# A three-block attention and expert kernel on one core: the first two tiles' softmax weights scaled by a product with a diagonal, first weight pieces split by VectorE, and the third tile's searches held behind the second tile

## The chip, the cores and the metric

The kernel runs on one core of a Trainium2 chip. The metric is the device time of one launch in microseconds (us), as the median of several runs. A profile shows one execution of it, engine by engine: TensorE (PE, with its weight loads PEld), VectorE (DVE), ScalarE (ACT), GpSimd (POOL) and SyncE (SP), which issues the transfers.

## The reference, cut to what matters

```python
# q, k, v: (2, 8, 576, 64); x has 1152 tokens of 512
scores = 0.125 * q @ k.T
mask = scores >= (32nd largest of each row)
attn = softmax over the kept scores
x = (attn @ v), heads side by side            # 1152 x 512
P = Sinkhorn scaling of exp(x @ w_gate)        # 1152 x 8
out = sum over 8 experts e of P[:, e] * (relu(x @ w1[e]) @ w2[e])
h = out @ w_in;  return (h * tanh(softplus(h))) @ w_out
```

## The kernel before

The 1152 tokens are nine tiles of 128 rows, counted from 0, in three chunks: (0, 1), (2, 3) and (4 to 8). For every tile and head, `scores` (L234) makes 128 x 576 scores on TensorE and ScalarE copies them out. `threshold` searches the 32 largest on VectorE: four times MAX8 (L262) and between them MATCH_REPLACE8 (L270). `mask` keeps the scores above the last one, and the exponentials; the weights lie in `em`. `norm` makes `r`, the reciprocal of the row's sum, on VectorE (L308, L309), and ScalarE multiplies `em` by it (L310). `values` turns the weights with four transposes against an identity (L330), for two heads together with a fifth for the 64 keys left (L341), ScalarE copies the result to `at` (L333) and `at2` (L344), and the product `pv` with the values follows (L353, L360). From `pv` ScalarE makes a rounded high part `xh` and VectorE the rest `xl`; for tile 1 each pair of heads has its own quarter (L367, L368).

The experts' passes take weights in pieces. For each piece `load_piece` fetches two halves `wraw0` and `wraw1`, ScalarE rounds them to `wh0` and `wh1` (L529), and GpSimd subtracts to get `wl0` and `wl1` (L533; VectorE takes a part of these in the last chunk). Three buffers hold the raw halves of each kind, so that the raw half of a piece is fetched when the split of the third piece before it is done. TensorE makes `h` from `xh`, `xl` and the pieces (L650), ScalarE and VectorE split it into `hh` and `hl` (L548, L549), and two pieces later `y` follows (L627). Expert 0 is done for tile 0 alone while tile 1's attention runs (`h_a`, L724, `y_a`, L710); the first chunk's pass then begins with expert 1, whose pieces are called `c0e1_0`, `c0e1_1` and so on.

TensorE's order is written by hand: the attention of tiles 2 and on is laid between the experts' products. The other engines' orders are set by a scheduler from priorities and its own estimate of times. `after(a, b)` adds a rule that `a` comes behind `b` in that order. The scores of tiles 2 and 3 are made early and wait in `early` stores. Tile 2's first MAX8 of a head is held behind `xl` of tile 1: heads 0 and 1 behind the quarter of pair 2, the others behind that of pair 3.

Of the kernel before, what the change touches and what calls it, by code (L numbers as in the profile page):

```python
# [10 lines left out]
F32 = mybir.dt.float32  # L11
F32R = mybir.dt.float32r
U32 = mybir.dt.uint32
AF = mybir.ActivationFunctionType
# [5 lines left out]
P = 128  # L20
B, H, S, D = 2, 8, 576, 64
# [5 lines left out]
NC = DM // P  # L27
# [13 lines left out]
CHUNKS = [(0, 1), (2, 3), (4, 5, 6, 7, 8)]  # L41
# [8 lines left out]
HOLD, RATE = 8, 0.25  # L50
ALONE, ALONE_RATE = 1, 3.4
FILL_FROM = 11
ROUND_AFTER = {f"c0e{ALONE}_0": H - 1, f"c0e{ALONE}_2": "v"}


class Streams:
# [19 lines left out]
def attention_moe_moe2(ctx: ExitStack, tc: tile.TileContext, qT, kT, vm, vt, wg, wst, w64, out):  # L76
    nc = tc.nc
# [5 lines left out]
    def after(inst, earlier):  # L83

        tc.add_manual_dep(
            inst.ins,
            earlier.ins.name,
            mybir.DependencyInfo(mybir.DependencyClass.NoSync, mybir.DependencyReason.DATA),
            reason="order",
        )  # L90
# [22 lines left out]
    hp = pool("hp", LAG + 1, stack=att)  # L113

    with st("attn"):
        ident = const.tile([P, P], F32, name="ident")
# [11 lines left out]
    xh, xl = {}, {}  # L128
# [24 lines left out]
    qset, live, away = {}, {}, {}  # L153
# [99 lines left out]
    def threshold(t, h, on_pool):  # L253

        with st("attn"):
            s = live["s", t, h]
            top = small.tile([P, TOPK], F32, tag="top", name=f"top_{t}_{h}")
            w = sp.tile([P, S], F32, tag="w", name=f"w_{t}_{h}")
            src = s
            for i in range(TOPK // 8):  # L260
                g = top[:, 8 * i : 8 * i + 8]
                top8 = nc.vector.max(g, src)  # L262
                if i == 0 and t == CHUNKS[0][-1] + 1:
                    key = 2 if h < 2 else 3
                    if ("xl", key) in live:
                        after(top8, live["xl", key])
                    else:
                        live.setdefault(("held", key), []).append(top8)
                if i + 1 < TOPK // 8:
                    nc.vector.match_replace(w, g, src, NEG)  # L270
                    src = w
            live["top", t, h] = top
            if not on_pool:
                live["e", t, h] = exponential(t, h, sp.tile([P, S], F32, tag="e", name=f"e_{t}_{h}"), s, nc.vector)
        yield from ()
# [27 lines left out]
    def norm(t, h, on_pool):  # L303
        with st("attn"):
            em, sm = live["em", t, h], live.pop(("sm", t, h))
            r = small.tile([P, 1], F32, tag="r", name=f"r_{t}_{h}")
            with st("moe" if on_pool else "attn"):
                nc.vector.tensor_scalar(r, sm, EPS, None, op0=ALU.add)  # L308
                nc.vector.reciprocal(r, r)  # L309
            nc.scalar.activation(em, em, AF.Copy, scale=r)  # L310
        yield from ()

    def turned(t, i, name):
# [7 lines left out]
    def values(t, h):  # L321
# [3 lines left out]
        j = h % 2  # L325
        with st("attn"):
            em = live.pop(("em", t, h))
            tr = turned(t, h, f"tr_{t}_{h}")
            for c in range(4):
                nc.tensor.transpose(tr[:, c, :], em[:, j * D + c * P :][:, :P], ident)  # L330
            at = sp.tile([P, 4, P], F32, tag="at", name=f"at_{t}_{h}", bufs=2)
            with st("evict"):
                nc.scalar.activation(at, tr, AF.Copy)  # L333
            live["at", j] = at
# [3 lines left out]
        pair = h // 2  # L338
        with st("attn"):
            tr2 = turned(t, 1, f"tr2_{t}_{h}")  # L340
            nc.tensor.transpose(tr2[:, 0, :], live.pop(("pair", t, h - 1))[:, 4 * P : 5 * P], ident)  # L341
            at2 = sp.tile([P, P], F32, tag="at2", name=f"at2_{t}_{h}")
            with st("evict"):
                live["copied", t, "v"] = nc.scalar.activation(at2, tr2[:, 0, :], AF.Copy)  # L344
        yield
        with st("attn"):
# [3 lines left out]
            for b, c0, c1, _, _ in queries(t, h // HG):  # L350
                for c in range(4):
                    for i in range(2):
# [4 lines left out]
                            start=(c == 0),  # L357
                            stop=False,
# [4 lines left out]
            ci, i = place[t]  # L363
            if t == CHUNKS[0][-1]:
                with st("first"):
                    hi, lo = (x[:, pair, i * P : (i + 1) * P] for x in x_tiles(ci))
# [4 lines left out]
            elif h == H - 1:  # L371
# [4 lines left out]
                hi, lo = (x[:, :, i * P : (i + 1) * P] for x in x_tiles(ci))  # L376
# [145 lines left out]
    def load_piece(tag, p, bufs2):  # L522
        res = []
        for a, (wp_a, bufs) in enumerate(((wp, 4), (wp if wq is None else wq, bufs2))):
            raw = wp.tile([P, DM], F32, tag=f"wraw{a}", name=f"wraw{a}_{tag}", bufs=3)
            nc.sync.dma_start(raw, p[:, a * DM : (a + 1) * DM])
            hi = wp_a.tile([P, DM], F32R, tag=f"wh{a}", name=f"wh{a}_{tag}", bufs=bufs)
            lo = wp_a.tile([P, DM], F32R, tag=f"wl{a}", name=f"wl{a}_{tag}", bufs=bufs)
            rounded = nc.scalar.activation(hi, raw, AF.Copy)  # L529
            if tag in ROUND_AFTER:  # L530
                after(rounded, live["copied", CHUNKS[0][-1], ROUND_AFTER[tag]])
            eng = nc.vector if (a and ps_b is not None) else nc.gpsimd
            eng.tensor_sub(lo, raw, hi)  # L533
            res.append((hi, lo))
        return res

# [403 lines left out]
```

## Time and profile before

| | us |
|---|---|
| median of 3 runs | 1217.76 |
| lowest, highest | 1215.89, 1219.01 |
| the profiled execution | 1214.06 |
| its span from first to last instruction | 1212.3 |

| engine | busy us | share of the span |
|---|---|---|
| TensorE | 1165.1 | 96% |
| VectorE | 853.6 | 70% |
| ScalarE | 652.9 | 54% |
| GpSimd | 514.2 | 42% |

The table of stages tells more than these shares: a stage is bounded by the engine that is busy all of it, or by the wait that ends last in it. In the timeline each row is a run of equal instructions on an engine: start, duration, what it is, and in brackets how long the engine idled before it and which instruction ended that. A row's duration includes the fill of the engine's pipeline, so equal rows overlap a little.

### The profile page before, as it was taken

What the parts mean: (1) busy time and instruction counts of PE and PEld (TensorE: products, weight loads), DVE (VectorE), ACT (ScalarE), POOL (GpSimd) and SP (SyncE); (2) the same over time, 40 slices, a digit from 0 to 9 for tenths busy, and PEclk for the clock granted to TensorE, in tenths of its full rate; (3) what the DMA queues carried; (4) which work ended last, traced back from release to release, by engine and by line L of the source; (5) the groups of instructions that cost most, each with busy time, mean ns of one, the idle gap of its engine ahead of it and who ended that gap; (6) DMA issues with size and microseconds to landing.
All of it is one profiled execution on the core that took longest, in us unless ns stands there. A gap on an engine that the chain in (4) does not pass through costs nothing.

```text
span 1212.3 us, 21068 instructions
## 1 busy us (share of the span) xinstructions
PE 1165.1 (96%) x7419; PEld 1042.2 (86%) x7419; DVE 853.6 (70%) x1868; ACT 652.9 (54%) x1305; POOL 514.2 (42%) x406
## 2 busy tenths in 40 slices
PE   3778999999999999999999999999999999999998
PEld 2556888988989899988999999999999999999997
DVE  7999999999999999913656868687576533333221
ACT  5877777876778777743223333333333334554432
POOL 6545778878787776752112121121211122221210
PEclk9999999999999999999999999999999999999999
DMA  8358566557665555544235666655444332223201
GB/s 251 115 184 261 177 184 183 175 179 222 186 201 164 159 167 164 176 144 144 71 94 177 201 189 196 195 183 182 151 140 147 119 102 64 88 96 117 76 27 44
DMA packets 105834, 184.68 MB, mean 152 GB/s; under 512 B 14208, under 2 KB 24704, under 8 KB 105728
## 3 DMA queue, kind: packets, MB, share of 16 engines
q1 hardware_dynamic: 104432, 182.15, 48.3%
q8 instruction: 58, 0.95, 0.3%
q10 hardware_dynamic: 1296, 1.18, 0.3%
q14 instruction: 48, 0.39, 0.1%
HBM read 159.43 MB, written 23.86 MB: 151 GB/s over the span
## 4 chain that ended last, share of the span: by engine, by line
PE 87%; DVE 6%; DMA 3%; ACT 2%; POOL 1%; issue 1%; SPq 0%; POOLq 0%; ACTq 0%
PE y_c2e L627 18%; PE h_c2e L650 18%; PE h_d L650 8%; PE y_d L627 8%; PE h_c1e L650 8%; PE y_c1e L627 8%; PE y_c0e L627 5%; PE h_c0e L650 5%; DVE top L262 3%; PE pv L353 2%; DMA kraw<-in_kT_dram 2%; PE tr L330 2%; DVE w L270 2%; PE sc L234 2%; PE pv L360 1%; DVE em L299 1%
## 5 line engine op out<-in xcount | busy, mean ns | idle before, releaser
L533 POOL TENSOR_TENSOR wl_c2e<-wraw_c2e,wh_c2e 128x512 fp32r<-128x512 f32 x64 | 84.2, 1316 | 348.4 <-ACT wh_c2e L529 348.4
L533 POOL TENSOR_TENSOR wl_c1e<-wraw_c1e,wh_c1e 128x512 fp32r<-128x512 f32 x128 | 171.2, 1348 | 60.1 <-ACT wh_c1e L529 57.2
L529 ACT ACTIVATE wh_c2e<-wraw_c2e 128x512 fp32r<-128x512 f32 x128 | 80.9, 632 | 194.6 <-PE y_c2e L627 100.6
L533 POOL TENSOR_TENSOR wl_c0e<-wraw_c0e,wh_c0e 128x512 fp32r<-128x512 f32 x112 | 149.9, 1356 | 42.1 <-ACT wh_c0e L529 37.7
L262 DVE MAX8 top<-w 128x8 f32<-128x576 f32 x216 | 158.6, 750 | 1.0
L650 PE MATMUL h_c2e<-xh,wh_c2e 128*128 128x256 f32 (+1 forms) x512 | 157.6, 308 | 1.3 <-DVE hl_c2e L549 1.3
L650 PE MATMUL h_c2e<-xl,wh_c2e 128*128 128x256 f32 (+1 forms) x512 | 157.1, 307 | 0.0
L650 PE MATMUL h_c2e<-xh,wl_c2e 128*128 128x256 f32 (+1 forms) x512 | 157.0, 307 | 0.0
L549 DVE SCALAR_TENSOR_TENSOR hl_c2e<-h_c2e,hh_c2e 128x256 fp32r<-128x256 f32 (+1 forms) x128 | 62.5, 489 | 98.9 <-ACT hh_c2e L548 98.4
L627 PE MATMUL y_c2e<-wh_c2e,hl_c2e 128*128 128x512 f32 x320 | 126.0, 394 | 0.0
L627 PE MATMUL y_c2e<-wh_c2e,hh_c2e 128*128 128x512 f32 x320 | 125.4, 392 | 0.0
L627 PE MATMUL y_c2e<-wl_c2e,hh_c2e 128*128 128x512 f32 x320 | 125.4, 392 | 0.0
L533 POOL TENSOR_TENSOR wl_d<-wraw_d,wh_d 128x512 fp32r<-128x512 f32 x32 | 41.5, 1296 | 160.5 <-ACT wh_d L529 160.5
L270 DVE MATCH_REPLACE8 w<-top,w 128x576 f32<-128x576 f32 x144 | 106.8, 743 | 0.0
L529 ACT ACTIVATE wh_c1e<-wraw_c1e 128x512 fp32r<-128x512 f32 x128 | 80.5, 629 | 47.2 <-PE y_c1e L627 22.0
L585 DVE TENSOR_TENSOR hl_d<-mg_d,hh_d 128x256 fp32r<-128x256 f32 x64 | 38.5, 602 | 91.9 <-ACT hh_d L584 91.9
L650 PEld LDWEIGHTS h_c2e<-xh,wh_c2e 128*128 128x128 f32 x512 | 96.2, 188 | 3.9 <-DVE hl_c2e L549 1.5
L650 PEld LDWEIGHTS h_c2e<-xl,wh_c2e 128*128 128x128 f32 x512 | 96.4, 188 | 2.5
L650 PEld LDWEIGHTS h_c2e<-xh,wl_c2e 128*128 128x128 f32 x512 | 96.2, 188 | 0.0
L529 ACT ACTIVATE wh_c0e<-wraw_c0e 128x512 fp32r<-128x512 f32 x112 | 70.1, 629 | 42.8 <-PE y_c0e L627 17.2
L234 PE MATMUL sc<-ks,q 128*128 128x288 f32 x320 | 65.3, 335 | 24.2 <-ACT s L243 4.9
L548 ACT ACTIVATE hh_c2e<-h_c2e 128x256 fp32r<-128x256 f32 (+1 forms) x128 | 54.7, 427 | 53.6 <-PE h_c2e L650 49.8
(171 smaller groups left out, 3313.8 us busy)
## 6 DMA issues: line engine op xcount, KB each, us to landing
wraw_c1e<-in_wst_dram SPq DMA_DIRECT2D x128, 256.0 KB, 3.0
wraw_c2e<-in_wst_dram SPq DMA_DIRECT2D x128, 256.0 KB, 3.0
wraw_c0e<-in_wst_dram SPq DMA_DIRECT2D x112, 256.0 KB, 3.0
cx<-in_w_dram SPq DMA_DIRECT2D x32, 512.0 KB, 4.2
wraw_d<-w SPq DMA_DIRECT2D x64, 256.0 KB, 2.6
yd<-ysp SPq DMA_DIRECT2D x32, 256.0 KB, 3.7
yb<-yd SPq DMA_DIRECT2D x32, 256.0 KB, 3.2
w<-cc SPq DMA_DIRECT2D x32, 256.0 KB, 3.5
```

The lines of the kernel that those rows point to most:

```text
L234: nc.tensor.matmul(halves[half], q[:, h % HG, :], ks[b, h][:, half * HS : (half + 1) * HS], start=(i == 0), stop=(i == len(terms) - 1),)
L262: top8 = nc.vector.max(g, src)
L270: nc.vector.match_replace(w, g, src, NEG)
L330: nc.tensor.transpose(tr[:, c, :], em[:, j * D + c * P :][:, :P], ident)
L353: nc.tensor.matmul(pv[i * D : (i + 1) * D, pair, c0:c1], vmain[b, pair][:, i, c, :], live["at", i][:, c, c0:c1], start=(c == 0), stop=False,)
L529: rounded = nc.scalar.activation(hi, raw, AF.Copy)
L533: eng.tensor_sub(lo, raw, hi)
L548: nc.scalar.activation(h, ps, AF.Relu)
L549: live["hl"] = nc.vector.scalar_tensor_tensor(l, ps, 0.0, h, op0=ALU.max, op1=ALU.subtract)
L585: nc.vector.tensor_sub(l, g, h)
L627: nc.tensor.matmul(y, h[:, j * P : (j + 1) * P], w, start=(f == 0 and k == 0), stop=(f == nf - 1 and k == 2),)
L650: nc.tensor.matmul(ps, w[:, c * P : (c + 1) * P], x[:, c, c0 : c0 + m], start=(k == 0), stop=(k == 3 * NC - 1),)
```

## The change

The kernel after differs in three things. For tiles 0 and 1, ScalarE no longer multiplies the weights by `r`; it multiplies the identity by it, which gives a 128 x 128 diagonal `turn`, and TensorE takes products of the weights with that diagonal where it took transposes. The fifth transpose of a pair becomes two products of 64 rows each. The order of expert 1's first three pieces is fixed anew: the subtractions for the first half of each go to VectorE, behind tile 1's last reciprocal; the roundings of the second halves, and of the third piece's first half, go behind tile 1's last copy, that of pieces 0 and 1's first halves behind the last head's copy of scores. And every first MAX8 of tile 2 is held behind the last quarter of tile 1's `xl`.

```diff
-ROUND_AFTER = {f"c0e{ALONE}_0": H - 1, f"c0e{ALONE}_2": "v"}
+FIRST_PIECES = {f"c0e{ALONE}_{f}": f for f in range(3)}
...
                 if i == 0 and t == CHUNKS[0][-1] + 1:
-                    key = 2 if h < 2 else 3
-                    if ("xl", key) in live:
-                        after(top8, live["xl", key])
+                    if ("xl", NC - 1) in live:
+                        after(top8, live["xl", NC - 1])
                     else:
-                        live.setdefault(("held", key), []).append(top8)
+                        live.setdefault(("held", NC - 1), []).append(top8)
...
-                nc.vector.reciprocal(r, r)
-            nc.scalar.activation(em, em, AF.Copy, scale=r)
+                inv = nc.vector.reciprocal(r, r)
+            if (t, h) == (CHUNKS[0][-1], H - 1):
+                live["ends"] = inv
+            if t > CHUNKS[0][-1]:
+                nc.scalar.activation(em, em, AF.Copy, scale=r)
+            else:
+                if h % 2 == 0:
+                    live["turn", t, h] = hp.tile([P, 2 * P], F32, tag="hl", name=f"turn_{t}_{h}")
+                turn = live["turn", t, h - h % 2][:, h % 2 * P :][:, :P]
+                nc.scalar.activation(turn, ident, AF.Copy, scale=r)
...
-                nc.tensor.transpose(tr[:, c, :], em[:, j * D + c * P :][:, :P], ident)
+                part = em[:, j * D + c * P :][:, :P]
+                if t > CHUNKS[0][-1]:
+                    nc.tensor.transpose(tr[:, c, :], part, ident)
+                else:
+                    nc.tensor.matmul(tr[:, c, :], part, live["turn", t, h - j][:, j * P :][:, :P], start=True, stop=True)
...
+                for i in range(2):
+                    keys = slice(i * D, (i + 1) * D)
+                    nc.tensor.matmul(tr2[keys, 0, :], tail[:, keys], turn[:, i * P :][:, :P], start=True, stop=True)
...
-            if tag in ROUND_AFTER:
-                after(rounded, live["copied", CHUNKS[0][-1], ROUND_AFTER[tag]])
             eng = nc.vector if (a and ps_b is not None) else nc.gpsimd
-            eng.tensor_sub(lo, raw, hi)
+            if tag in FIRST_PIECES:
+                late = a or FIRST_PIECES[tag] == 2
+                after(rounded, live["copied", CHUNKS[0][-1], "v" if late else H - 1])
+            if tag in FIRST_PIECES and not a:
+                after(nc.vector.tensor_sub(lo, raw, hi), live["ends"])
+            else:
+                eng.tensor_sub(lo, raw, hi)
```

VectorE behind tile 1's last reciprocal (`r_1_7`), in the kernel before; `top_2_0` is tile 2's head 0, `xl0` the low part of tile 1, whose four quarters have one name:

```order
L309 RECIPROCAL r_1_7_1254<-r_1_7_1254 128x1
L368 TENSOR_TENSOR xl0_806<-pv_1_1065,xh0_805 128x128
L262 MAX top_2_0_1239<-early_xh2_326 128x8
L262 MAX top_2_1_1265<-early_xh2_326 128x8
L270 MATCH_REPLACE w_2_0_1240<-top_2_0_1239,early_xh2_326 128x576
L280 TENSOR_SCALAR nb_2_0_1249<-top_2_0_1239 128x1
L270 MATCH_REPLACE w_2_1_1266<-top_2_1_1265,early_xh2_326 128x576
L280 TENSOR_SCALAR nb_2_1_1275<-top_2_1_1265 128x1
L262 MAX top_2_0_1239<-w_2_0_1240 128x8
L262 MAX top_2_1_1265<-w_2_1_1266 128x8
L270 MATCH_REPLACE w_2_0_1240<-top_2_0_1239,w_2_0_1240 128x576
L368 TENSOR_TENSOR xl0_806<-pv_1_1065,xh0_805 128x128
```

The quarter of pair 2 comes first, then nine instructions of tile 2's search, then the quarter of pair 3. VectorE at the same place in the kernel after:

```order
L308 RECIPROCAL r_1_7_1269<-r_1_7_1269 128x1
L553 TENSOR_TENSOR wl0_c0e1_0_1326<-wraw0_c0e1_0_1323,wh0_c0e1_0_1325 128x512
L553 TENSOR_TENSOR wl0_c0e1_1_1355<-wraw0_c0e1_1_1352,wh0_c0e1_1_1354 128x512
L386 TENSOR_TENSOR xl0_814<-pv_1_1076,xh0_813 128x128
L553 TENSOR_TENSOR wl0_c0e1_2_1384<-wraw0_c0e1_2_1381,wh0_c0e1_2_1383 128x512
L386 TENSOR_TENSOR xl0_814<-pv_1_1076,xh0_813 128x128
L262 MAX top_2_0_1254<-early_xh2_327 128x8
L262 MAX top_2_1_1280<-early_xh2_327 128x8
L262 MAX top_2_2_1523<-early_xh2_327 128x8
L262 MAX top_2_3_1628<-early_xh2_327 128x8
L269 MATCH_REPLACE w_2_0_1255<-top_2_0_1254,early_xh2_327 128x576
L279 TENSOR_SCALAR nb_2_0_1264<-top_2_0_1254 128x1
```

Three subtractions for expert 1's pieces stand among the quarters, and all of tile 2's search behind the last of them. The next instruction there is the first `hl` of expert 1. ScalarE behind tile 1's last copy (`at2_1_7`), in the kernel before:

```order
L344 ACTIVATE at2_1_7_1294<-tr2_1_7_1292 128x128
L529 ACTIVATE wh0_c0e1_2_1367<-wraw0_c0e1_2_1365 128x512
L529 ACTIVATE wh1_c0e1_2_1373<-wraw1_c0e1_2_1371 128x512
L529 ACTIVATE wh0_c0e1_3_1404<-wraw0_c0e1_3_1402 128x512
L281 ACTIVATE e_2_0_1248<-early_xh2_326,nb_2_0_1249 128x576
L367 ACTIVATE xh0_805<-pv_1_1065 128x128
```

and in the kernel after:

```order
L362 ACTIVATE at2_1_7_1310<-tr2_1_7_1307 128x128
L547 ACTIVATE wh0_c0e1_2_1383<-wraw0_c0e1_2_1381 128x512
L547 ACTIVATE wh0_c0e1_3_1420<-wraw0_c0e1_3_1418 128x512
L547 ACTIVATE wh1_c0e1_0_1331<-wraw1_c0e1_0_1329 128x512
L547 ACTIVATE wh1_c0e1_1_1360<-wraw1_c0e1_1_1358 128x512
L547 ACTIVATE wh1_c0e1_2_1389<-wraw1_c0e1_2_1387 128x512
L385 ACTIVATE xh0_813<-pv_1_1076 128x128
```

Between the last copy and the rounding of the last quarter stand five roundings of weights where three and an exponential stood. TensorE's order is the same in both kernels, but for the operands of the changed products. GpSimd's first subtraction for expert 1 is `wl0_c0e1_3`.

## Rows read from the trace of the kernel before

**Rows 1.** Stages: us, then each engine's busy us, TensorE's clock, DMA share, GB/s.

```profile
core 0: us, PE busy (x) PEld busy (x) DVE busy (x) ACT busy (x) POOL busy (x), PEclk, DMA share, GB/s
60.00:91.00 31.00, 23.21 (x158) 18.34 (x158) 30.79 (x77) 24.75 (x59) 12.27 (x13) 1.00 0.59 188
91.00:101.00 10.00, 10.00 (x75) 7.80 (x74) 9.86 (x22) 7.21 (x17) 4.28 (x4) 1.00 0.74 233
127.00:210.00 83.00, 83.00 (x600) 73.86 (x601) 82.92 (x214) 61.49 (x122) 65.66 (x50) 1.00 0.60 182
210.00:1212.00 1002.00, 996.38 (x6286) 901.09 (x6284) 654.78 (x1377) 497.90 (x982) 376.53 (x286) 1.00 0.46 144
```

**Rows 2.** Timeline of TensorE, 90 to 127 us: start, us, instruction, [idle before, releaser].

```profile
96.93 1.05 PE L724 MATMUL h_a<-x_alone,wraw_a 128*128 128x128 f32 x8
...
102.37 1.09 PE L353 MATMUL pv<-at,vm 128*64 128x128 f32 x16
104.38 0.49 PE L360 MATMUL pv<-at,vt 128*128 128x128 f32 x2 [0.92 <-ACT at L344]
104.71 1.04 PE L330 MATMUL tr<-ident,em 128*128 128x128 f32 x8
...
106.06 1.57 PE L353 MATMUL pv<-at,vm 128*64 128x128 f32 x16 [0.20 <-ACT at L333]
...
107.89 1.04 PE L330 MATMUL tr<-ident,em 128*128 128x128 f32 x8
...
109.98 1.57 PE L353 MATMUL pv<-at,vm 128*64 128x128 f32 x16 [0.95 <-ACT at L333]
...
111.73 0.37 PE L650 MATMUL h_c0e<-xh,wh_c0e 128*128 128x256 f32 x1
...
114.44 0.39 PE L650 MATMUL h_c0e<-xl,wh_c0e 128*128 128x256 f32 x1 [1.04 <-DVE xl L368]
...
117.54 0.38 PE L650 MATMUL h_c0e<-xh,wh_c0e 128*128 128x256 f32 x1 [1.18 <-DVE nb L280]
...
126.85 0.38 PE L650 MATMUL h_c0e<-xh,wh_c0e 128*128 128x256 f32 x1 [0.77 <-DVE hl_c0e L549]
```

**Rows 3.** Timeline of VectorE, 99 to 118 us.

```profile
99.14 1.70 DVE L299 SCALAR_TENSOR_TENSOR em<-s,top,e 128x576 f32<-128x576 f32 x1
...
105.78 0.81 DVE L299 SCALAR_TENSOR_TENSOR em<-s,top,e 128x576 f32<-128x576 f32 x1
...
106.82 0.16 DVE L309 RECIPROCAL r<-r 128x1 f32<-128x1 f32 x1
108.95 0.29 DVE L368 TENSOR_TENSOR xl<-pv,xh 128x128 fp32r<-128x128 f32 x1 [1.98 <-ACT xh L367]
...
114.10 0.29 DVE L368 TENSOR_TENSOR xl<-pv,xh 128x128 fp32r<-128x128 f32 x1
...
117.06 0.43 DVE L549 SCALAR_TENSOR_TENSOR hl_c0e<-h_c0e,hh_c0e 128x256 fp32r<-128x256 f32 x1
```

**Rows 4.** Timeline of ScalarE, 103 to 113 us.

```profile
103.41 0.76 ACT L310 ACTIVATE em<-em,r 128x576 f32<-128x576 f32 x1
...
110.45 1.69 ACT L529 ACTIVATE wh_c0e<-wraw_c0e 128x512 fp32r<-128x512 f32 x3
...
112.68 0.28 ACT L367 ACTIVATE xh<-pv 128x128 fp32r<-128x128 f32 x1
```

**Rows 5.** The chain of waits in order of time: start, us, what.

```profile
52.62 0.66 ACT em L310
```

**Rows 6.** Transfers issued from 100 to 116 us: count, size, median us to landing.

```profile
wraw_c0e<-in_wst_dram SPq DMA_DIRECT2D x11, 256.0 KB, 5.3
```

**Rows 7.** Line L533 on VectorE: count, least, median and greatest ns, first and last start.

```profile
L533 DVE TENSOR_TENSOR wl_c2e<-wraw_c2e,wh_c2e x64: 680/686/693, 543.1 to 979.8; 128x512 fp32r<-128x512 f32 x64
```

**Rows 8.** Timeline at tile 3's first head, on VectorE and on TensorE.

```profile
183.79 0.14 DVE L309 RECIPROCAL r<-r 128x1 f32<-128x1 f32 x1
...
186.66 0.60 PE L330 MATMUL tr<-ident,em 128*128 128x128 f32 x4
```

More of the change, by code (lines that the diff above doesn't have):

```diff
@@ L340, in values @@
             tr2 = turned(t, 1, f"tr2_{t}_{h}")
-            nc.tensor.transpose(tr2[:, 0, :], live.pop(("pair", t, h - 1))[:, 4 * P : 5 * P], ident)
+            tail = live.pop(("pair", t, h - 1))[:, 4 * P : 5 * P]
+            if t > CHUNKS[0][-1]:
+                nc.tensor.transpose(tr2[:, 0, :], tail, ident)
+            else:
+                turn = live.pop(("turn", t, h - 1))
+                for i in range(2):
+                    keys = slice(i * D, (i + 1) * D)
+                    nc.tensor.matmul(tr2[keys, 0, :], tail[:, keys], turn[:, i * P :][:, :P], start=True, stop=True)
             at2 = sp.tile([P, P], F32, tag="at2", name=f"at2_{t}_{h}")
@@ L529, in load_piece @@
             rounded = nc.scalar.activation(hi, raw, AF.Copy)
-            if tag in ROUND_AFTER:
-                after(rounded, live["copied", CHUNKS[0][-1], ROUND_AFTER[tag]])
             eng = nc.vector if (a and ps_b is not None) else nc.gpsimd
-            eng.tensor_sub(lo, raw, hi)
+            if tag in FIRST_PIECES:
[3 more added lines that the diff above has]
+                after(nc.vector.tensor_sub(lo, raw, hi), live["ends"])
+            else:
+                eng.tensor_sub(lo, raw, hi)
             res.append((hi, lo))
```

## The prediction, as it was made before the result

> **What bounds the kernel now.** I read the table by stages first [rows 1]. From 210 us to the end TensorE is busy 996.4 of 1002 us, and from 127 to 210 us all of it; a change to the first two tiles can reach the end only by the moment at which TensorE gets into that stretch, or by a wait that it opens inside it. In the same 83 us from 127 to 210 VectorE is busy 82.9: it works on the searches of tiles 2 and 3 (tiles are counted from 0 here, so the "third tile" is tile 2) and has nothing to spare. From 91 to 101 us TensorE is full too (10.00 of 10), while from 60 to 91 it is busy 23.2 of 31.
>
> Then TensorE in order of time between 90 and 127 us [rows 2]: six waits, 0.92, 0.20, 0.95, 1.04, 1.18 and 0.77, 5.06 us together. They are all that the change can win there. Last VectorE and ScalarE in the same stretch [rows 3, 4]: the last reciprocal of tile 1 is made at 106.82, VectorE idles 1.98 us, makes one quarter of tile 1's low part at 108.95, then searches for tile 2 and only at 114.10 makes the last quarter, for which TensorE waits at 114.44.
>
> **Products instead of transposes.** Four transposes of a head are four instructions, four fp32 products are eight: eight of either take the same 1.04 and 1.05 us [rows 2], so each is near 0.11 us and a head costs 0.44 us more. The tail goes from one instruction to four of 64 rows; sixteen such take 1.09 us with their fill, so 0.26 instead of 0.11, +0.15 a pair (+0.33 if the halves don't overlap). For 16 heads and 8 pairs that is 7.0 + 1.2 = 8.2 us more TensorE work. Tile 0's half lies before 91 us, where TensorE idles 7.8 us of 31 [rows 1] and where waits for others end last: taken as nothing, at most 4.1. Tile 1's half is on the path.
>
> The Trainium skill, "TensorE: Matmul & The Clock Gate", section "Terms", calls the transpose mode 4x faster for FP32; the eight-instruction group of [rows 2] shows 2x for this shape, and I go by the row. By the page tile 1's heads would pay 1.32 instead of 0.44 each; that is a rival below.
>
> **Scaling a diagonal instead of the weights.** ScalarE gives up 0.76 us a head for 128 columns, which take it 0.28 [rows 4]: 0.5 us back, 16 times. Three of the old scalings of tile 0 stand in the chain of waits, the last of them at 52.62 [rows 5], so at most 1.5 us could be won ahead of 60 us. VectorE runs without a pause between there and 91, and TensorE is full from 91, with more work than before; I take 0.2.
>
> **Tile 1, step by step.** Heads 1 to 3 and two tails come ahead of the product for pair 1 that starts at 102.37: 3 x 0.44 + 2 x 0.15 = 1.62, so 103.99. Its length 1.09 ends at 105.08; the wait of 0.92 at 104.38 is gone, because the tail's copy stood behind a 0.76 scaling [rows 4]. Net +0.70. Heads 4, 5 and a tail add 1.03: the next product, 1.15 us after the transposes without its wait of 0.20, comes at 105.41 + 1.15 + 1.03 = 107.6 instead of 106.06; ScalarE's copy of the doubled head ends near 107.9, so between, 107.7. The next transposes come at 109.5 instead of 107.89; with 1.14 us (2.09 less the wait of 0.95) and 1.03 more, pair 3 starts at 111.7, and with the copy behind it about 111.8 instead of 109.98. Expert 1's first product then starts at 113.5 instead of 111.73, **+1.8 us**. Two of the waits vanish and the added work outweighs them.
>
> **ScalarE's queue in front of the last quarter.** After tile 1's last copy, at about 112.1, the order now holds five roundings of weight pieces and only then the rounding of the last quarter; before it held three and an exponential. Three took 1.69 [rows 4], five take 2.7: 114.8, then 0.28 and 0.29 for the high and low part [rows 3, 4]: 115.3. One of the five needs a raw piece that can be fetched only after VectorE's split at 107 (its buffer is freed by that), and a fetch takes 5.3 us in this stretch [rows 6]: 112.9, when its turn is at 112.6. Up to 1 us late; I take 115.5 for the end of the last quarter, bounds 114.3 (as now) and 116.4.
>
> **Splits on VectorE.** Three at 0.69 [rows 7], 2.1 us. Two lie in VectorE's present 1.98 us of idling, the third in the wait for ScalarE: nothing. If that cover were gone, 2.1. GpSimd's queue gets three subtractions shorter; the next pieces come no later for that.
>
> The Trainium skill, "GPSIMD Engine Reference", section "Key points", says that GpSimd shares its SBUF interfaces with VectorE and collides with instructions that have two SBUF inputs. Here a masking instruction beside a GpSimd subtraction took 1.70, and 0.81 alone [rows 3]; so the trace agrees. By it the third split could take 0.89 longer; the order of GpSimd has its first subtraction behind a rounding that comes after that split's, so I take nothing.
>
> **The held searches.** This is the term that decides. Before, the first search of tile 2 started right behind the quarter at 108.95, about 109.16, and between there and 114.10 VectorE did nine instructions of that search, seven of them long ones at about 0.69 us. Now all of tile 2 waits for the last quarter: 115.5 instead of 109.16, less the 0.19 of that quarter itself, which stood among them: VectorE is **6.15 us late** with tiles 2 and 3, and it has no idle time up to 210 to make it up [rows 1]. On VectorE the low part of expert 1's first piece now stands behind four maxima and one replacement (five at 0.69, 3.4 us), so 118.9 instead of 117.06 [rows 3]: TensorE's wait of 1.18 goes to the same kind of wait, 1.8 later.
>
> How late may VectorE be? Tile 3's first weights have their reciprocal at 183.93 and, with 0.77 for the scaling, stand ready 2.0 us ahead of TensorE at 186.66 [rows 8]. TensorE's order is unchanged there, so 6.15 - 2.0 = **4.15 us** of wait lands in a stretch where TensorE had none. The 1.8 us of the tile-1 part is not added: both measure the same lateness, and the larger rules. After 210 TensorE is full; with 0.2 from tile 0, +4.0.
>
> **Sum.** The profiled execution took 1214.06 us (span 1212.3 and 1.8 around it): 1214.06 + 4.0 = 1218.1. The median of the three runs, 1217.76, lies 3.7 above that execution; the same step on it gives **1221.8**. About 0.3% (3.65 us) is what a measurement of this kernel can tell from no change, so the forecast is a slight slowing at the edge of it.
>
> **Rivals.** A: VectorE's lateness is mostly swallowed. For: ScalarE's scalings of tiles 2 and 3 stand behind other work on its queue, so orders that shift a little can find slack, and GpSimd's shorter queue makes masking faster (up to 0.89 an instruction). With the last quarter at 114.3 lateness is 4.95; less 2.0 and 0.9 it costs 2, 1219.8: within 0.3%. Against: [rows 1] show no idle time. B, the other side: tile 1's part decides and VectorE doesn't. If the early 1.5 us carries to 91, all 5.06 us of waits go and only 1.62 of the products shows, the end comes 4.9 earlier, 1212.9. The point from which it decides is a lateness under 2.0, a last quarter before 111.4, when its product hasn't started; so hardly. C: lateness is paid twice, because expert 1's low parts stand in the same VectorE order as the searches and each late one stops TensorE as at 126.85: 6.15 without slack and 0.5 more, 1224.4. D: the product costs four times a transpose: seven heads at 0.88 more, +6.2, 1228; the row speaks against it. That the change doesn't do what it says is ruled out by the order, where splits, products and the hold all stand.
>
> **Chances.** Forecast 0.48, A 0.40, B 0.05, C 0.06, D 0.01. Slower by over 0.3%: forecast, C and D, 0.55; within: 0.40; faster: 0.05. The range reaches from just below no change, which holds A, to a little over C with the spread of the runs: 1217.4 to 1225.4.
>
> **What would show it.** Eight instructions for each head's product; VectorE idle about 7 us in all between 106 and 116, its first tile-2 search at 115 to 116; TensorE's waits at 104 and 110 gone, one of about 2 us before expert 1's third piece, and new waits of together some 3 us between 130 and 200 at the transposes of tiles 2 and 3 for ScalarE's scaling. After 210 the two traces should run at a constant distance. I am wrong if the searches start before 112, or if TensorE shows no new wait between 130 and 200.

## The result, and the profile after it

The changed kernel takes 1226.03 us (median of five runs, 1223.04 to 1229.25) against 1217.76 of the kernel before; these two medians differ by 8.3. The ratio on record is 1.0081, interval 1.0067 to 1.0096, so 8.2 to 11.7 us slower, 9.9 in the middle; the differences below are all taken from such ratios. The forecast was slower, by 4.0 us, 1221.8, and its range ended at 1225.4: the direction was right, the size less than half. (Below, a thousandth of the ratio is 1.2 us.) The profiled execution took 1228.52 us, span 1226.7.

The stages after, as [rows 1] before (us, then each engine's busy us with its instructions, TensorE's clock, DMA share, GB/s):

```profile
core 0: us, PE busy (x) PEld busy (x) DVE busy (x) ACT busy (x) POOL busy (x), PEclk, DMA share, GB/s
60.00:91.00 31.00, 24.49 (x166) 19.50 (x165) 29.45 (x74) 20.21 (x54) 13.48 (x12) 0.94 0.51 164
91.00:101.00 10.00, 8.99 (x68) 6.96 (x67) 8.28 (x21) 6.96 (x18) 1.80 (x2) 1.00 0.68 200
127.00:210.00 83.00, 77.18 (x540) 67.30 (x539) 82.99 (x196) 57.33 (x112) 62.59 (x48) 0.98 0.56 169
210.00:1226.00 1016.00, 1010.66 (x6386) 913.22 (x6384) 669.49 (x1418) 510.04 (x1002) 388.57 (x294) 1.00 0.46 144
```

From 127 to 210 us TensorE had 83.00 of 83 before; now it has 77.18, and part of that at a lower clock, while VectorE is as full as it was. From about 200 us on the two traces run at nearly a constant distance: the transposes that the kernel before makes at 202 us come 14.2 us later, its products at 451 us 14.9 and those at 565 us 14.4 us later (this execution is 2.5 us over its median, that of before 3.7 under).

TensorE at the places that the forecast named, as [rows 2] before:

```profile
113.43 1.09 PE L371 MATMUL pv<-at,vm 128*64 128x128 f32 x14 [0.17 <-ACT at L344]
...
118.73 0.36 PE L672 MATMUL h_c0e<-xh,wh_c0e 128*128 128x256 f32 x1
...
124.48 0.38 PE L672 MATMUL h_c0e<-xh,wh_c0e 128*128 128x256 f32 x1 [1.84 <-DVE hl_c0e L571]
...
140.74 0.29 PE L427 MATMUL lg<-ident,lt 16*128 16x16 f32 x2 [2.65 <-ACT lt L422]
140.96 0.78 PE L649 MATMUL y_c0e<-wh_c0e,hh_c0e 128*128 128x512 f32 x1
141.54 0.63 PE L649 MATMUL y_c0e<-wl_c0e,hh_c0e 128*128 128x512 f32 x1
...
145.26 0.66 PE L339 MATMUL tr<-ident,em 128*128 128x128 f32 x4 [1.39 <-ACT em L312]
```

The waits of 0.92 and 0.95 in tile 1 are gone but for 0.17, as foreseen; expert 1's first product stands at 118.73 instead of 111.73; the new wait before its third piece is 1.84. Then come two things that were not foreseen: a wait of 2.65 us at the gate's logits, and behind it a product of 512 columns that takes 0.63 to 0.78 us instead of 0.39. VectorE shows where the first comes from:

```profile
111.72 0.16 DVE L308 RECIPROCAL r<-r 128x1 f32<-128x1 f32 x1
...
115.28 0.29 DVE L386 TENSOR_TENSOR xl<-pv,xh 128x128 fp32r<-128x128 f32 x1 [2.21 <-ACT xh L385]
118.14 0.69 DVE L553 TENSOR_TENSOR wl_c0e<-wraw_c0e,wh_c0e 128x512 fp32r<-128x512 f32 x1 [2.56 <-ACT wh_c0e L547]
120.38 0.29 DVE L386 TENSOR_TENSOR xl<-pv,xh 128x128 fp32r<-128x128 f32 x1 [1.55 <-ACT xh L385]
120.59 2.73 DVE L262 MAX8 top<-early_xh 128x8 f32<-128x576 f32 x4
...
133.54 4.60 DVE L298 SCALAR_TENSOR_TENSOR em<-early_xh,top,e 128x576 f32<-128x576 f32 x1
...
138.80 0.80 DVE L298 SCALAR_TENSOR_TENSOR em<-early_xh,top,e 128x576 f32<-128x576 f32 x1
```

The hold is there: 6.3 us of idling, then the first search of tile 2 right behind the last quarter. But the masking of tile 2's head 0 takes 4.60 us, the next one 0.80. GpSimd and ScalarE in the same stretch:

```profile
118.70 18.82 POOL L555 TENSOR_TENSOR wl_c0e<-wraw_c0e,wh_c0e 128x512 fp32r<-128x512 f32 x15 [14.46 <-ACT wh_c0e L547]
139.56 1.28 POOL L555 TENSOR_TENSOR wl_c0e<-wraw_c0e,wh_c0e 128x512 fp32r<-128x512 f32 x1 [2.04 <-ACT wh_c0e L547]
```

```profile
138.18 0.78 ACT L280 ACTIVATE e<-early_xh,nb 128x576 f32<-128x576 f32 x1 [2.91 <-DVE em L298]
...
140.33 0.36 ACT L422 ACTIVATE lt<-lt 16x256 f32<-16x256 f32 x1
```

GpSimd stands for 14.46 us, because its first subtraction's rounded piece now comes behind the end of tile 1; then it has 15 subtractions in a row, up to 118.70 + 18.82 = 137.52. The masking that starts at 133.54 ends at 138.14, 0.62 us after the row. ScalarE's next exponential waits 2.91 for it, the copy of the gate's logits stands behind that exponential, and TensorE waits for the copy. The granted clock then is 0.50, the lower level of 1.2 GHz:

```profile
140.00:141.00 1.00, 0.26 (x3) 0.23 (x3) 1.00 (x4) 1.00 (x3) 0.84 (x1) 1.00 0.00 0
141.00:144.00 3.00, 2.87 (x7) 1.76 (x6) 3.00 (x10) 0.64 (x4) 1.28 (x1) 0.50 0.45 102
```

So there were two questions: which part of the change costs how much, and how much of it is this masking.

### The profile page after: what moved, and what is told of

Its sections match the earlier page's. It is cut to its first block, busy times and chain, and to the rows that moved or that the text cites. A ratio compares the mean times of both kernels' runs of the same rounds, so it can differ in the third digit from the quotient of the medians.

```text
span 1226.7 us, 21247 instructions
## 1 busy us (share of the span) xinstructions
PE 1178.6 (96%) x7507; PEld 1053.4 (86%) x7507; DVE 859.4 (70%) x1871; ACT 650.2 (53%) x1305; POOL 511.2 (42%) x403
## 4 chain that ended last, share of the span: by engine, by line
PE 84%; DVE 7%; ACT 2%; issue 1%; DMA 1%; POOL 0%; ACTq 0%; POOLq 0%; SPq 0%
PE y_c2e L649 18%; PE h_c2e L672 18%; PE h_d L672 8%; PE y_d L649 8%; PE h_c1e L672 8%; PE y_c1e L649 8%; PE y_c0e L649 4%; PE h_c0e L672 4%; DVE top L262 2%; PE pv L371 2%; DVE w L269 2%; PE tr L339 2%; PE sc L234 2%; DVE em L298 1%; PE pv L378 1%
## 5 line engine op out<-in xcount | busy, mean ns | idle before, releaser
L555 POOL TENSOR_TENSOR wl_c0e<-wraw_c0e,wh_c0e 128x512 fp32r<-128x512 f32 x109 | 146.3, 1361 | 54.9 <-ACT wh_c0e L547 48.6
```

## Experiments

**The changed kernel again**, for a second profile.

> The changed kernel once more, for a second profile of it. The first profile showed the distance to the kernel before grow in three places: +1.9 us at 76 us (tile 0), +4.9 at 91 us (a wait of 2.12 us and a stretch of half clock behind it), +7.0 at expert 1's first product, and +8 more between 130 and 175 us, where one masking took 4.60 us beside 15 GpSimd subtractions in a row and the granted clock was 0.50 for some 3 us. If these belong to the kernel, the second profile has them at the same instructions: masking of tile 2's head 0 over 3 us, GpSimd without a subtraction from 104 to 118. If they belong to that one execution (its 1228.5 us is 2.5 over the median), the masking takes 0.8 to 1.9 us and the distance after 175 us is 9 to 11 us. Time by either: 1226, between 1223 and 1229.

Measured: 1227.2 us, ratio 1.0081 (1.0062 to 1.0099). The second profile has the same masking, wait and clock (0.50 from 139 to past 144 us), so they belong to the kernel:

```profile
116.99 2.73 DVE L262 MAX8 top<-early_xh 128x8 f32<-128x576 f32 x4
...
129.92 4.60 DVE L298 SCALAR_TENSOR_TENSOR em<-early_xh,top,e 128x576 f32<-128x576 f32 x1
```

```profile
137.11 0.29 PE L427 MATMUL lg<-ident,lt 16*128 16x16 f32 x2 [2.56 <-ACT lt L422]
```

What differs are the first 110 us: expert 1 starts 3.6 us earlier here, and 1.7 of that are there at 62 us already, where the second profile is as early as that of the kernel before. The distance of the first profile at 119 us is therefore not all the change's; against the kernel before, the second has expert 1's first product 3.40 us later (115.13 and 111.73).

**The three parts, alone and left out.** only_H is the kernel before with the hold, only_P with the products, only_S with the splits (the held roundings belong to them); no_P, no_H and no_S are the changed kernel with one part undone.

```diff
# only_H, on the kernel before
-                    key = 2 if h < 2 else 3
-                    if ("xl", key) in live:
+                    if ("xl", NC - 1) in live:
...
# no_H, on the changed kernel: the same lines back
```

```diff
# only_P, on the kernel before (tails and scaling alike, as in the change)
-                nc.tensor.transpose(tr[:, c, :], em[:, j * D + c * P :][:, :P], ident)
+                    nc.tensor.matmul(tr[:, c, :], part, live["turn", t, h - j][:, j * P :][:, :P], start=True, stop=True)
...
# no_P, on the changed kernel: transposes and scaled em back
```

```diff
# only_S, on the kernel before
-            if tag in ROUND_AFTER:
-                after(rounded, live["copied", CHUNKS[0][-1], ROUND_AFTER[tag]])
+                after(rounded, live["copied", CHUNKS[0][-1], "v" if late else H - 1])
+                after(nc.vector.tensor_sub(lo, raw, hi), live["ends"])
...
# no_S, on the changed kernel: ROUND_AFTER and GpSimd's subtractions back
```

> The kernel before with the hold alone: every first search of tile 2 behind the last quarter. Theory 1, VectorE's lateness decides (the step of the forecast): VectorE starts tile 2 about 5 us late, about 2 of them are slack, +3 us, 1220.8. Theory 2, the products decide: within 1 us of before, 1217.8. Theory 3, the held roundings leave GpSimd with a row of subtractions that blocks VectorE's masking: the hold alone moves no rounding, so +3 at most, and no masking over 2 us in the trace.

> The kernel before with the products alone (tiles 0 and 1). Theory 1: +0.8 us (forecast by its steps for tile 1: 1.8 later at expert 1's first product, mostly swallowed), 1218.6. Theory 2, the products decide, in tile 0 too, where I had taken them as free: the first profile shows +1.9 at 76 us and +1.6 more from 91 to 107, so +3.5 to +5, 1221 to 1223. Theory 3: no more than theory 1.

> The kernel before with the splits alone (three subtractions on VectorE and the first pieces' roundings held to the end of tile 1). Theory 1: 0 to +1 us, 1218. Theory 2: the same. Theory 3: GpSimd has no subtraction from about 100 to 112 us, then a row of 12 or more without a gap, and the masking of tile 2's head 0 takes over 3 us if it falls into the row; +2 to +5, 1220 to 1223. With the hold undone the masking comes 5 us earlier, deeper in the row, so theory 3 lets it take even longer than 4.6 us.

> The changed kernel without the products (transposes and scaled weights back, splits and hold kept). The hold alone measured 1.0030 of before, the splits alone 1.0003, the products alone 1.0082, the whole change 1.0081. Theory 2 (the products decide): what is left is at most the hold, 1.000 to 1.004 of before, 1216 to 1221. Theory 3 (held roundings make GpSimd's row, which blocks the masking): splits and hold together put the masking of tile 2's head 0 late into the row, over 3 us long, and the time is 1.005 or more, with no product in it.

> The changed kernel with the hold undone (products and splits). Theory 1 (the hold's lateness of VectorE, my forecast's step, costs 4): 1222, 1.004 of before. Theory 2 (the products decide and the hold hides behind them): as after, 1.007 to 1.009, 1225 to 1227.

> The changed kernel with the splits undone (products and hold; the roundings held as before). Theory 2: as the products alone, 1.008, 1226. Theory 3: the row of 15 subtractions is broken, the masking of tile 2's head 0 takes under 2 us, and the time is 3 to 5 us under that of the changed kernel, 1221 to 1223. If parts simply added, products and hold would give 1.011, 1230.

Measured:

| kernel | products | splits | hold | ratio (interval) | us |
|---|---|---|---|---|---|
| only_S | | x | | 1.0003 (0.9993 to 1.0013) | +0.4 |
| only_H | | | x | 1.0030 (1.0017 to 1.0043) | +3.6 |
| only_P | x | | | 1.0082 (1.0066 to 1.0099) | +10.0 |
| no_P | | x | x | 1.0038 (1.0021 to 1.0054) | +4.6 |
| no_H | x | x | | 1.0043 (1.0026 to 1.0060) | +5.2 |
| no_S | x | | x | 1.0075 (1.0060 to 1.0090) | +9.1 |
| changed | x | x | x | 1.0081 (1.0067 to 1.0096) | +9.9 |

The splits cost nothing alone. The hold costs 3.6 alone and 4.2 on top of the splits (4.6 - 0.4), and in the place that the forecast named: in no_P TensorE waits 3.2 us at the transposes of tiles 2 and 3, and VectorE's first search stands at 115.38. The products cost 4.8 on top of the splits (5.2 - 0.4) and 5.3 on top of splits and hold (9.9 - 4.6): this is where most of the missing time lies. Each of these differences has an interval of about 2.5 us to either side. Alone the products cost 10.0, twice as much, and the splits give half of that back. The trace of only_P shows part of the reason; TensorE's and ScalarE's timelines:

```profile
112.71 1.09 PE L372 MATMUL pv<-at,vm 128*64 128x128 f32 x14 [1.55 <-ACT at L345]
...
121.01 0.38 PE L669 MATMUL h_c0e<-xh,wh_c0e 128*128 128x256 f32 x1 [1.72 <-ACT xh L386]
122.10 0.58 PE L669 MATMUL h_c0e<-xl,wh_c0e 128*128 128x256 f32 x1 [0.71 <-DVE xl L387]
122.48 0.42 PE L669 MATMUL h_c0e<-xh,wl_c0e 128*128 128x256 f32 x1
```

```profile
111.55 0.63 ACT L548 ACTIVATE wh_c0e<-wraw_c0e 128x512 fp32r<-128x512 f32 x1 [0.87 <-DMA wraw_c0e<-in_wst_dram]
...
113.64 0.63 ACT L548 ACTIVATE wh_c0e<-wraw_c0e 128x512 fp32r<-128x512 f32 x1 [0.82 <-DMA wraw_c0e<-in_wst_dram]
```

With the roundings in their old places ScalarE waits twice for a raw piece ahead of tile 1's copies, and TensorE waits for ScalarE (1.55); later it waits 1.72 and 0.71, and behind 122 us, at a granted clock of 0.50, a product of 256 columns takes 0.42 to 0.58 instead of 0.28. Holding the roundings to the end of tile 1 removes the first of these; all waits of TensorE from 100 to 210 us come to 7.9 us in only_P and to 3.9 in no_H.

Of the theories, the first held for only_H, and the second for only_S, no_P and no_S, though not for only_P, whose 10.0 us none of the three foretold; no_H, 1.0043, came out as the first says. The third, that the held roundings alone make a row of subtractions that blocks the masking, failed twice. The masking of tile 2's head 0 and GpSimd's row in only_S, then in no_P:

```profile
123.85 0.99 DVE L299 SCALAR_TENSOR_TENSOR em<-early_xh,top,e 128x576 f32<-128x576 f32 x1
...
112.51 22.80 POOL L539 TENSOR_TENSOR wl_c0e<-wraw_c0e,wh_c0e 128x512 fp32r<-128x512 f32 x17 [11.82 <-ACT wh_c0e L531]
```

```profile
129.27 1.35 DVE L298 SCALAR_TENSOR_TENSOR em<-early_xh,top,e 128x576 f32<-128x576 f32 x1
...
113.49 21.30 POOL L538 TENSOR_TENSOR wl_c0e<-wraw_c0e,wh_c0e 128x512 fp32r<-128x512 f32 x16 [12.43 <-ACT wh_c0e L530]
```

Both maskings start inside a row of 17 or 16 subtractions without a gap and take 0.99 and 1.35, where more than 4.6 and over 3 were expected. So such a row is not enough to make the masking long.

**Which tile's products.** Splits, no hold, and the products in one tile only; and in place of products every transpose made twice.

```diff
# S_P0 (S_P1): the changed kernel without the hold; at the three places
-                if t > CHUNKS[0][-1]:
+                if t != 0:          (t != 1)
# S_twice: splits, no products
+                for _ in range(2 if t <= CHUNKS[0][-1] else 1):
                     nc.tensor.transpose(tr[:, c, :], em[:, j * D + c * P :][:, :P], ident)
```

> Splits and tile 0's products, no hold, tile 1 with transposes. Splits alone measured 1.0003 of before, splits and both tiles' products 1.0043, that is 5 us for the products. My forecast took tile 0's part as hidden (its own step: nothing, at most 4.1): then 1216 to 1217. If tile 0 carries part of the 5 us (the profiles show the distance growing between 62 and 91 us): 1218 to 1220.

> Splits and tile 1's products, no hold, tile 0 with transposes. By my forecast's steps tile 1's part puts expert 1 1.8 us later: 1218. If tile 1 carries all of the products' 5 us: 1221. If tile 0 and tile 1 share them: 1218 to 1220, and S_P0 and this add up to about 5 us.

> Splits, no products: each transpose of tiles 0 and 1 is made twice into the same place, the scaling of the weights stays on ScalarE as before. TensorE does the same number of instructions for a head as with the products, four 128x128 more each. If the products cost by TensorE's time: as splits and products together, 1.004, 1220 to 1221, or a little more, since ScalarE's 0.5 us a head isn't won. If the products cost by what they wait for or by what ScalarE does: under 1218.

Measured: S_P0 0.9996 (0.9983 to 1.0009), S_P1 1.0038 (1.0024 to 1.0052), S_twice 1.0074 (1.0060 to 1.0087). Tile 0's products are free, as the forecast took them; all of the cost is tile 1's, 4.2 us over the splits. The trace of S_P1 names two places. TensorE at 82 to 85 us and expert 1's first product, in S_P0, S_P1 and only_S:

```profile
83.04 1.16 PE L747 MATMUL h_a<-x_alone,wraw_a 128*128 128x128 f32 x8
...
111.93 0.36 PE L673 MATMUL h_c0e<-xh,wh_c0e 128*128 128x256 f32 x1
```

```profile
84.10 1.16 PE L747 MATMUL h_a<-x_alone,wraw_a 128*128 128x128 f32 x8 [2.07 <-ACT early L247]
...
115.72 0.36 PE L673 MATMUL h_c0e<-xh,wh_c0e 128*128 128x256 f32 x1
```

```profile
84.64 1.16 PE L730 MATMUL h_a<-x_alone,wraw_a 128*128 128x128 f32 x8 [0.94 <-ACT early L247]
...
112.55 0.36 PE L656 MATMUL h_c0e<-xh,wh_c0e 128*128 128x256 f32 x1
```

Expert 1's first product comes 3.79 us later than in S_P0 and 3.17 later than in only_S, which differs from S_P1 in tile 1's products alone (the first 40 us of these executions differ by up to 1.3 us). About 1.1 of that is a longer wait for ScalarE ahead of the product at 84 us, 2.07 instead of 0.94; with tile 0's products, in S_P0, that wait is gone. S_twice, of which 1220 to 1221 was expected, takes 1226 and costs more than the products, though for a head's four blocks it gives TensorE the same number of instructions: it leaves ScalarE its scalings. That TensorE's time alone makes the cost is not shown by it, only that it can't be had for nothing.

**A gap in GpSimd's row.** GpSimd copies the sum of tile 2's head 0, and two subtractions stand behind that copy, so that GpSimd is still while VectorE masks. gap writes the copy into a new tile of one column, gap64 into one of 16, gap_warm into a column that is there already; pad32 is the changed kernel with the new tile of one column and nothing else; old_round has the roundings held as before.

```diff
# gap (gap64: [P, 16]; gap_warm: no tile, the copy goes into warm)
+                if (t, h) == (2, 0):
+                    seen = small.tile([P, 1], F32, tag="seen", name="seen", bufs=1)
+                    live["seen"] = nc.gpsimd.tensor_copy(seen, sm)
...
+                if (tag, a) in (("c0e1_7", 1), ("c0e2_0", 0)):
...
+                        after(sub, live["seen"])
# pad32: at the start
+        seen = small.tile([P, 1], F32, tag="seen", name="seen", bufs=1)
+        nc.gpsimd.memset(seen, 0.0)
# old_round
-                after(rounded, live["copied", CHUNKS[0][-1], "v" if late else H - 1])
+                if FIRST_PIECES[tag] != 1:
+                    after(rounded, live["copied", CHUNKS[0][-1], "v" if FIRST_PIECES[tag] == 2 else H - 1])
```

> The changed kernel with a gap put into GpSimd's row: one copy of 128x1 on GpSimd that reads the sum of tile 2's head 0, and two subtractions behind it, so that GpSimd stands still at the moment of that masking. If the masking takes 4.60 us because GpSimd's row has no gap: 0.8 to 1.3 us here, ScalarE's exponential and the copy of the gate's logits some 3 us earlier, TensorE's wait of 2.6 us at the gate's logits and the half clock behind it gone, 3 to 5 us faster than the changed kernel, 1221 to 1223. If the masking is long for its own sake: 4.6 us here too. If the products decide the time in another way (alone they cost 10 us with no masking over 1.9 us), the masking is short and the time stays within 2 us of the changed kernel, 1224 to 1228.

> As gap, but the small tile that GpSimd's copy writes has 16 columns instead of one. In gap the masking was short (0.81 us) and the waits at the gate's logits gone, yet the whole run was 8 us over the changed kernel: from 120 us to 1020 us one 512-column product started every 232.5 ns instead of 229.0, in waits of nobody. The tile of one column had moved every tile behind it by 32 bytes (addresses in a partition are given out in steps of 32); with 16 columns they move by 64. If the slow pace comes from the addresses: 229.0 again here and the gain of the gap shows, 4 to 5 us under the changed kernel, 1221 to 1222. If it comes from the GpSimd copy or its wait: 232.5 again, 1234.

> As gap, but GpSimd's copy writes into a column that is there already and not used any more, so no tile moves. If the masking of 4.60 us is on the path: it takes 0.8 to 1.3 us here, TensorE's wait at the gate's logits and the half clock behind it are gone, one 512-column product every 229.0 ns as in the changed kernel, and the time is 4 to 5 us under the changed kernel, 1221 to 1222 (1.0045 of before). If VectorE's lateness rules without it: 1224 to 1226 with a short masking. If the copy on GpSimd itself slows TensorE: 232 ns again and 1231 to 1234.

> The changed kernel with one unused column of a pool in front of most tiles (set to zero at the start), which moves them by 32 bytes as in gap; no copy, no gap. If the slow pace of gap comes from the addresses: 232 ns for a 512-column product here, from 120 to 1020 us, and about 10 us more than the changed kernel, 1234 to 1237. If it came from the copy or the gap: 229.0 ns, 1226.

> The changed kernel with the roundings of the first pieces held as before (products, hold and the three subtractions on VectorE kept). GpSimd's first subtraction of expert 1 then needn't wait for the end of tile 1. If the held roundings make the row that blocks the masking: GpSimd starts some 7 us earlier, its row has gaps when the masking of tile 2's head 0 comes, which takes under 2 us, and the time is 3 to 5 us under the changed kernel, 1221 to 1223. Against it: the products without the held roundings measured 1.0075 (with the hold) and 1.0082 (without), since ScalarE then stands in front of tile 1's copies and waits for raw pieces: then 1225 to 1227 with a short masking.

Measured: gap 1.0143 (1.0124 to 1.0162), gap64 1.0120 (1.0106 to 1.0135), gap_warm 1.0057 (1.0045 to 1.0070), pad32 1.0162 (1.0145 to 1.0178), old_round 1.0072 (1.0058 to 1.0086).

gap_warm settles the masking. Its VectorE, its GpSimd, and all that TensorE waits for from 127 to 210 us (us in total, times, longest):

```profile
132.57 0.86 DVE L298 SCALAR_TENSOR_TENSOR em<-early_xh,top,e 128x576 f32<-128x576 f32 x1
...
134.09 1.47 DVE L298 SCALAR_TENSOR_TENSOR em<-early_xh,top,e 128x576 f32<-128x576 f32 x1
```

```profile
117.76 15.05 POOL L559 TENSOR_TENSOR wl_c0e<-wraw_c0e,wh_c0e 128x512 fp32r<-128x512 f32 x12 [14.40 <-ACT wh_c0e L551]
133.50 0.19 POOL L300 COPY warm<-sm 128x1 f32<-128x1 f32 x1 [0.69 <-DVE em L298]
133.64 6.81 POOL L559 TENSOR_TENSOR wl_c0e<-wraw_c0e,wh_c0e 128x512 fp32r<-128x512 f32 x5
```

```profile
PE tr L343 <- ACT em L316: 3.0, 2, 1.6
PE tr L343 <- ACT at L348: 0.2, 1, 0.2
```

One copy of 0.19 us on GpSimd, and the masking takes 0.86 instead of 4.60, the wait at the gate's logits is gone, and with it the half clock. The time falls from 1.0081 to 1.0057, 2.9 us. The interval of that difference is about 2.3 to either side, and the expectation of 4 to 5 was too high; the 3.0 us of waits at the transposes, which belong to the hold, stay. What is left, 6.9 us, is 2.3 over no_P, which is within the intervals of both.

gap and gap64 have the same short masking (0.81 and 0.90) and are slower all the same, and pad32, which has no gap (its masking takes 4.48), is 1.0162. TensorE's instructions in the same 220 us of the third chunk, changed kernel, then pad32, then gap64, then no_H:

```profile
660.00:880.00 220.00, 220.00 (x1246) 200.32 (x1245) 161.40 (x276) 78.75 (x149) 41.78 (x32) 1.00 0.59 187
```

```profile
660.00:880.00 220.00, 220.00 (x1226) 198.64 (x1225) 159.39 (x272) 76.70 (x147) 41.60 (x32) 1.00 0.59 184
```

```profile
660.00:880.00 220.00, 220.00 (x1236) 200.35 (x1236) 160.07 (x274) 77.78 (x149) 40.77 (x32) 1.00 0.59 186
```

```profile
660.00:880.00 220.00, 220.00 (x1235) 200.35 (x1235) 157.53 (x270) 77.34 (x148) 40.40 (x31) 1.00 0.58 184
```

No wait, full clock, and 1.6% fewer products in pad32. One more column is enough: gap's loss came with the tile, not with its copy or the gap. That it is the move of the other tiles' addresses is a likely reason and not shown: no run here records an address, gap64 came out neither as the one expectation had it nor as the other, and no_H and no_P, which add no tile, have 1235 products in these 220 us as well. In the profile of no_H the same roundings of `hh_c2e` stand 7.8 us behind those of the kernel before at 627 us and 10.7 at 903, in no_P 8.0 and 10.9, in the other kernels without a new tile they keep their distance. So up to 2.9 us of what no_H and no_P cost (5.2 and 4.6 in the table) can be this pace and not the parts; how many of their executions have it, the record doesn't say (no_H's nine lie between 1219.91 and 1226.19, and the profiled one took 1224.75).

old_round breaks the row as well: GpSimd starts at 110.99, and the masking takes 1.35. Yet it costs 1.0072, because ScalarE then waits for raw pieces in tile 1 again (TensorE waits 1.6 us for its copies there, as it did in only_P). It removes one cost and brings back another, so of the row it shows only that it hangs on the held roundings.

## Why the forecast was too small

**Right.** VectorE's order decides, as forecast: the hold alone costs 3.6 us (2.1 to 5.2). Tile 0's products: nothing (S_P0, -0.5 with an interval of -2.1 to +1.1). The splits: nothing (+0.4, -0.9 to +1.6). Two instructions for one [rows 2]: eight products of a head take 1.05 to 1.06; rival D, four times a transpose, is out by the same row. The five roundings in front of the last quarter: 2.7 forecast, 2.71 in both profiles. Some 3 us of new waits at the transposes of tiles 2 and 3: 3.0.

**The step that failed** is "so 6.15 - 2.0 = **4.15 us** of wait", in both of its terms, and a third term, the masking, was put at nothing.

The 6.15 was too small. It holds the products of tile 1 already: the 112.1 from which it is worked out has the roundings behind the last copy 1.65 us later than the 110.45 of the kernel before [rows 4]. So it was right not to add the 1.8 of the tile-1 part again; but 1.8 was too little. In the second profile, whose first 62 us are as fast as before, the last reciprocal comes at 108.25 instead of 106.82, the five roundings start at 113.87 instead of 112.1, and the first search of tile 2 stands at 116.99 instead of 115.5: 7.8 us later than the 109.16 of before. ScalarE's row there:

```profile
113.87 2.71 ACT L547 ACTIVATE wh_c0e<-wraw_c0e 128x512 fp32r<-128x512 f32 x5
```

Expert 1's first product is 3.4 us later there, and 3.2 to 3.8 in S_P1. I had started to count at 91 us, where tile 1's heads 1 to 3 come, and had called everything before hidden; about 1.1 us of it is the wait at 84 us.

The slack of 2.0 wasn't there. I read it at one head, tile 3's first, and from the reciprocal, as if ScalarE scaled at once; in [rows 8] the reciprocal is at 183.79, but the scaling starts only at 184.57, so the lead was 1.3. Two heads later, in the kernel before, it is 0.9 (198.59 and 0.77 for the first of two scalings, against 200.24):

```profile
198.59 1.44 ACT L310 ACTIVATE em<-em,r 128x576 f32<-128x576 f32 x2
...
200.24 0.60 PE L330 MATMUL tr<-ident,em 128*128 128x128 f32 x4
```

And the runs show about none. In only_H the first search stands here:

```profile
113.02 2.73 DVE L262 MAX8 top<-early_xh 128x8 f32<-128x576 f32 x4
```

That is 3.9 us later than 109.16, and the first chunk's last rounding of `hh_c0e` starts at 316.9 instead of 313.1, 3.8 later. The two distances are 6.2 and 7.3 in no_P, 10.5 and 11.6 in no_S, 11.0 and 12.0 in old_round, 10.5 and 9.9 in gap_warm (each counted from its own start); in the second profile of the changed kernel 7.8, and 3.8 for the long masking, stand against 11.8. With the hold, VectorE's lateness at the first search reaches the end of the chunk within about 1 us.

That the hold measured 3.6 and 4.2 beside a forecast of 4.15 is therefore partly luck: without the products the forecast's own steps put the last quarter's end at 113.7, so 4.4 us of lateness and, less 2.0, 2.4 of cost.

**The missing term: the masking**, 2.9 us (changed against gap_warm, 0.6 to 5.2). I had the row that priced it (1.70 beside a GpSimd subtraction, 0.81 alone, [rows 3]) and used it in the wrong direction: rival A counts GpSimd's shorter queue as faster masking. The roundings that the splits hold back let GpSimd stand for 14.46 us and then run 15 subtractions in a row, and the first masking comes into that row. I took one subtraction as the most that a masking can meet; here it met the rest of one and three whole ones. gap_warm shows that the row is needed for it; only_S and no_P show that a row is not enough.

With 7.8 of lateness, no slack and 2.9 for the masking the same sum gives 10.7 instead of 4.15, and 9.9 was measured. The differences of neighbouring kernels (splits 0.4, hold 4.2, products on top 2.3, masking 2.9) add up to 9.8, but by construction, and the pace of no_P makes its 4.6, and with it the 4.2 and the 2.3, uncertain.

**The clock** was no term of the forecast. Behind 62 us it fell to 0.50 in the first profile in two places, after waits of 2.12 us (at 85.5) and 2.65; in the second only at the latter, and in gap_warm at neither. Its cost is within the masking's 2.9 where it follows the 2.65, and I can't split it off.

**Of the rivals** A is out: what VectorE is late is not swallowed, it reaches the end. C, lateness paid twice, 1224.4, was nearest in time, and right that there is no slack, but its reason was another: expert 1's low parts stopped TensorE once (1.84, foreseen), and later for 0.2 more. B, the other side, was wrong: its 5.06 us of waits did shrink, and the products took more than that.

**Left open.** The products seem cheaper on top of the hold (2.3) than without it (4.8). Two things in the traces go that way: without the hold the last quarter itself is late, so that no_H and S_P1 wait 1.7 and 1.5 us for its high and low part, against 0.4 and nothing in the changed kernel, and the clock is 0.50 from 122 to 128 us behind that; and the pace of no_H and no_P raises the 4.8 and lowers the 2.3. Nor does any kernel here take away the wait at 84 us alone. No version beat the kernel before; S_P0 is level with it.

## What to carry to other kernels

A lead that is read at one instruction is not the slack of a stretch: look for the least lead among all places at which one engine feeds the other, and from the instruction that really runs last. An edit that ties an engine's start to the end of a stage turns every cost of that stage into a cost behind it. When work on a helper engine is held back, ask what its queue looks like when it is let go: a pile without gaps can stop an engine that runs beside it, as a pause around one copy of 0.19 us showed by giving 2.9 us back. And an experiment that adds a tile can change the pace of the whole kernel: write into one that is there, measure the tile by itself, and compare the pace of a stretch without waits before a difference of two kernels is put down to the edit.

## What was not expected of the hardware

A masking of VectorE (two inputs in SBUF, 128x576) waited through a row of GpSimd subtractions: 4.60 us, and 4.60 again in the second profile, where 0.80 is its time alone, with its end 0.62 us behind the end of the row. The Trainium skill, "SBUF — State Buffer", section "SBUF: two separate sides", says that of a GpSimd instruction and a VectorE instruction with two SBUF inputs whichever starts first has the shared pair of ports for the whole instruction and that the other blocks fully. The traces agree on the blocking, and go further: it lasted not for one instruction but for what was left of the row. In gap_warm the masking of 1.47 us ends at 135.56, inside five subtractions without a gap, and in only_S and no_P maskings of 0.99 and 1.35 us stand inside rows of 17 and 16, so VectorE does get in between two of them at times. In the three profiles with the long masking (the changed kernel twice, and pad32) it starts 0.15, 0.12 and 0.08 us before the next subtraction starts, in only_S and no_P 0.34 and 0.87 us before it; whether that decides it was not tried.

One more tile of one column slowed TensorE's products by 1.6% in a stretch in which it waits for nothing (1226 instead of 1246 in 220 us), and the whole run by 9.9 us (1.0162 against 1.0081); with 16 columns it was about half of that in the same stretch (1236). That the tile moves the others' addresses, by 32 or 64 bytes, is not recorded, and no_H and no_P have 1235 in that stretch without any new tile; the cause is open.
